# One inverse moved to GpSimd, the later pairs' scans put off by one pair, and a block of MLP pieces placed ahead of the fifth pair

## The chip, the core and the metric

The kernel runs on one core of one Trainium2 chip. The metric is the device time of one execution in microseconds. The engines are named as the profile names them: PE (TensorE; PEld is its weight load), DVE (VectorE), ACT (ScalarE), POOL (GpSimd) and SP (SyncE, which issues most transfers). Each engine takes its instructions in the order in which they stand in its own queue.

## The reference: a recurrence and two MLPs

Inputs are six arrays r, k, v, w, a, b of 4 batches x 8 heads x 768 steps x 40. Per batch and head a 40 x 40 state is carried over the steps:

```python
y[t]  = r[t] @ state
Sa    = state @ a[t]
state = state * w[t][None, :] - outer(Sa, b[t]) + outer(v[t], k[t])
```

The outputs y of all heads are joined to x (3072 tokens x 320). The first MLP normalises x by its root mean square, computes `silu(xn @ w_gate) * (xn @ w_val) @ w_out` with an inner width of 1536. The second computes `(h - tanh(h)) @ w_out2` with `h = x @ w_in2` and an inner width of 2048. All is float32.

## The kernel before: pairs of chunks, an inverse per group of pairs, MLP pieces in between

**Recurrence.** The 768 steps are cut into chunks of 64. A unit is one batch and one chunk (all 8 heads); two units make a pair, and there are 24 pairs, counted here from 0, so that "the fifth pair" is pair 4. A loop `for p in range(NP + 1)` (L826) goes over the pairs. In each turn of it PE computes the right-hand side (`emit_rhs`, L397), the outputs of the pair before (`emit_y`, L505 and L507), the first solve (`emit_u`, L408), a correction (`emit_w`, L417; DVE adds it at L418), the second solve (`emit_u2`, L425) and then the state's update and the products for the output. A solve multiplies by TT, the inverse of a triangular 64 x 64 matrix that is loaded by `load_t` (L347).

**What has to be there before a solve.** A unit's inputs are loaded into the arena (`load_p`, L203); DVE runs two scans over them (`emit_p`, L218 and L222), POOL makes three products (L228 to L230), and they are spilled (L234). `emit_m` (L247) then makes the pair's matrices on PE, which go to DRAM as `md`. Pairs are inverted in groups: (0,1), (2,3), (4,5), (6,7), (8 to 11), (12 to 15), (16 to 19), (20 to 23), here group 0 to group 7. `inverse` loads a group's matrices from `md` (L270), runs 31 steps of two instructions each, a product into tmp (L276) and a subtraction (L278), which makes 62 instructions, each needing the one before, and stores the result as `td` (L282). `load_t` reads `td`. Groups 0, 1 and 3 run on DVE, the others on POOL. All groups but group 1 (tile mt) use the same place in the arena. When a group's last pair has its matrices, `m_due` puts its inverse into `held`, and it is run at the end of that turn of the loop. A dictionary `AHEAD` says which pairs' scans are begun in which turn: before, pairs 4, 5, 6 in turns 0, 1, 2, then two pairs in each of the turns 3 to 5, and p + 7 from then on. At turn 18 and later a turn that has no inverse in `held` begins splits of the second MLP's weights (`some2`).

**Weights.** Products are made of rounded high and low parts. `split_words` splits a block of 128 rows of weights: an absolute value on ACT, five instructions on DVE (L141, L142, L143, L145, L146), a copy on ACT, two on POOL (L150, L151). The first MLP has 48 such blocks (6 chunks of 8), the second 40. The tile fa, which a block holds from ACT's first instruction to POOL's last one, has three buffers; raw, the words as loaded, has four.

**First MLP.** It runs in 12 blocks of 256 tokens, one for every two pairs, cut into pieces: an up piece (8 matmuls at L556; two make one of 12 slices f) and a down piece (6 matmuls, L561 to L563, per f, two slices behind). `moe(RATE)` (L768) is called about nine times in a turn and puts in as many pieces as its credit allows. Where no block is ready it puts in 8 matmuls on a tile of zeros instead, which are called fillers here (`warm`, L288). A block can begin when its two pairs have been normalised (`emit_x1`: ACT, POOL at L516 and L517, DVE at L518, POOL at L519; stored to DRAM), loaded again and transposed (`emit_x2`).

**What sets the order.** PE's order is written out by the program as it stands. The order on DVE, ACT, POOL and SP comes from a list scheduler: each instruction gets a priority (`when`, `step`, `later`), and the scheduler places it by its own reckoning of times. What stands in a queue is therefore fixed before the run, and an instruction that has to wait holds all that stand behind it.

Of the kernel before, what the change touches and what calls it, by code (L numbers as in the profile page):

```python
# [20 lines left out]
HC = C // 2  # L21
NCH = S // C
NU = B * NCH
NP = NU // 2
# [5 lines left out]
UNITS = [(b0 + g, c) for b0 in range(0, B, G) for c in range(NCH) for g in range(G)]  # L30
GROUPS = [(g, g + 2) for g in range(0, 8, 2)] + [(g, g + 4) for g in range(8, NP, 4)]

AHEAD = {3: (7, 8), 4: (9, 10), 5: (11, 12)}
KEEP = 2
NPO = 6
NPE = 8
NRAW = 4
NFA = 3
EARLY1 = 2
# [19 lines left out]
AR_P = HC * HC * 2  # L59
# [9 lines left out]
def wkv_chunks__then__gated_mlp__then__tanh_mlp_kernel(  # L69
# [269 lines left out]
    def load_t(p):  # L339
        if p >= NP:  # L340
            return
        gi = group_of[p]
        x = p - GROUPS[gi][0]
        for s in range(2):
            for h in range(2):
                r0 = 64 * s + 32 * h
                SP.dma_start(out=TT[r0:r0 + HC, :, :, 32 * h:32 * h + HC].rearrange("p w q t -> p (w q) t"),  # L347
                             in_=td_d[gi][h, x, s].rearrange("w q j t -> j (w q) t"))
# [277 lines left out]
    with tc.manual_schedule(engines={mybir.EngineType.PE}):  # L626
# [30 lines left out]
        mt = fp.tile([128, AR_P], F32, tag="mt", name="mt")  # L657

        with tc.manual_schedule(engines={ET.DVE, ET.SP, ET.Activation, ET.Pool}):
            when(-100)  # L660
            for u in range(4):
                load_p(u, fp)
            SP.dma_start(out=idn, in_=ident)
            SP.dma_start(out=msk, in_=masks[1:2].rearrange("o p t -> p o t"))
            for u in range(4, NPO):
                load_p(u, fp)
            DVE.memset(z65, 0.0)
            DVE.memset(z65[:, :, 0:1], 1.0)
            DVE.memset(zr, 0.0)
            for t in (turn[0], turn[1], gapped, solve, wz):  # L670
                DVE.memset(t, 0.0)
            i0 = inverse(0, DVE, MA, TA, fp)
            i1 = inverse(1, DVE, mt[:, 0:HC * HC], mt[:, HC * HC:AR_P], fp)
            next(i0)
            POOL.memset(EP, 0.0)
            POOL.memset(cm05, -0.5)
            for u in range(4):
                emit_p(u, fp)
                if u % 2:
                    emit_m(u // 2, fp)  # L680
            for t in (Q, VS, UV, MX, TT):
                DVE.memset(t, 0.0)
            POOL.memset(RU, 0.0)
            load_kl(0)
            load_q(0)
            load_v(0)
            load_r(0)
            next(i0)
            load_mx(0)
            for u in range(6, 8):  # L690
                load_p(u, fp)
            emit_s(0)
            emit_p(4, fp)
            emit_p(5, fp)
            for w in range(2):
                emit_kb(0, w)
            load_e(0)
            next(i1)
            for k in range(HC - 1):
                if k == 8:  # L700
                    emit_mak(0)
                if k == 18:
                    emit_rhs(0)
                next(i0)
            emit_m(2, fp)
            spill_p(4, SP)
            run(i0)
            first_w = lastd[0]
            load_t(0)
            spill_p(5, SP)  # L710
            warm(WARM0)
            emit_p(6, fp)
            emit_p(7, fp)
            SP.dma_start(out=gB, in_=rms_g.rearrange("(o n) -> o n", o=1).to_broadcast([128, DM]))
            spill_p(6, SP)
            spill_p(7, SP)
# [109 lines left out]
        for p in range(NP + 1):  # L826
            period[0] = p
            now, more = p < NP, p + 1 < NP
            if now:
                scans.extend(2 * q + w for q in AHEAD.get(p, (p + 4 if p < 3 else p + 7,)) if q < NP for w in range(2))  # L830
            if p == 1:
                for u in range(2 * KEEP):
                    po_t.pop(u)
                    sp_t.pop(u)
                last_t = lastd[0]
                first.close()
                w1p = phA.enter_context(tc.tile_pool(name="w1p", bufs=1, side="right", reuse_waits="tile"))
                with tc.issue_after(last_t.ins):
                    prep1(range(EARLY1, KF1 // 2), w1p)
                when(vt[0])  # L840
                pairs.close()
                ma = phA.enter_context(tc.tile_pool(name="ma", bufs=2, side="right", reuse_waits="tile"))
            if now and p:
                emit_rhs(p)
                load_q(p + 1)
            if p:
                emit_y(p - 1)
                load_r(p)
                later(X_LATE, emit_x1, p - 1)
            step(1.8)  # L850
            moe(RATE)
            if now:
                emit_u(p)
                if p == 0:
                    load_q(1)
                    emit_m(3, fp)
                    when(0)
                    run(i1)
                    when(vt[0])
                else:  # L860
                    m_due()
                step(1.2)
                moe(RATE)
                emit_w(p)
                if more:
                    if p + 1 not in kl_t:
                        load_kl(p + 1)
                    load_mx(p + 1)
                    emit_kb(p + 1, 0)
                stage_p()  # L870
                step(1.2)
                moe(RATE)
                emit_u2(p)
                emit_ut(p)
                load_t(p + 1)
                if more:
                    emit_kb(p + 1, 1)
                step(1.9)
                moe(RATE)
                emit_d(p)  # L880
                load_v(p + 1)
                stage_p()
                step(0.8)
            if p > 1:
                x2()
                step(0.5)
            moe(RATE)
            if now:
                for w in range(2):
                    emit_z(p, w)  # L890
                    step(0.8)
                    moe(RATE)
                if more:
                    emit_mak(p + 1)
                    if p + 2 < NP:
                        load_kl(p + 2)
                    emit_s(p + 1)
                if scans:
                    m_due()
                    stage_p()  # L900
                step(1.5)
                moe(RATE)
                emit_e(p)
                load_e(p + 1)
                if scans:
                    stage_p()
                step(0.4)
            if p > 1:
                x2()
                step(0.5)  # L910
            moe(RATE)
            if held:
                with tc.issue_after(gate[0].ins), tc.issue_after(gate_pool[0].ins):
                    later(I_LATE, run, held.pop(0))
            elif p >= 18:
                some2()
        with tc.issue_after(gate[0].ins), tc.issue_after(gate_act[0].ins):
# [130 lines left out]
```

## Time and profile before

| | us |
|---|---|
| median of 2 runs (1435.42 to 1435.57) | 1435.49 |
| the profiled execution's own time | 1433.76 |
| its span from the first to the last instruction | 1432.0 |
| PE busy in the span | 1233.9 |
| DVE busy | 717.1 |
| POOL busy | 707.7 |
| ACT busy | 469.4 |

The span leaves 1.76 us of the profiled execution's time outside it, and the execution is 1.73 us under the median of the runs. In a row of the timeline stand the start, the time taken, engine, source line, operation, tiles written and read, shapes and count; in square brackets how long the engine sat idle before, and what ended that. A row of the groups has the busy time, the mean of one in ns, and the idle time before. Instructions of one engine that follow each other closely can overlap in a row of matmuls, since their ends are modelled.

### The profile page before, as it was taken

Reading aid. Unit: us, or ns where it says so; the run is one execution under the profiler, and the core shown is the slowest. Engines: PE = TensorE matmul, PEld = TensorE weight load, DVE = VectorE, ACT = ScalarE, POOL = GpSimd, SP = SyncE. Lnnn points to the kernel's source line nnn. Section 1 sums busy time; section 2 is a strip of 40 time slices with the busy share of each in tenths; the row PEclk is TensorE's granted clock in tenths of the full one; section 3 lists DMA queues with packets and bytes.
Section 4 is the critical chain, followed back from the end, with each engine's and each line's share of the span. In section 5 each row is a group of like instructions: output and inputs, shape, how many; then the busy total and the mean of one; then the engine's idle time right before and its main releaser. Section 6 shows DMA issues by size and latency. Waiting matters only on the chain.

```text
span 1432.0 us, 35619 instructions
## 1 busy us (share of the span) xinstructions
PE 1233.9 (86%) x14676; PEld 1139.0 (80%) x14676; DVE 717.1 (50%) x1487; ACT 469.4 (33%) x1077; POOL 707.7 (49%) x1049
## 2 busy tenths in 40 slices
PE   2666676279889989998999899998877999999997
PEld 1555566278789979998999898988766999899997
DVE  5989899563434434443443344435978222222221
ACT  1132332123223323333333233333434333333332
POOL 5554788533683395349425622324767333333332
PEclk9888678589999999999999999999999999999999
DMA  8476765444755645565544334332331101010000
GB/s 211 103 178 155 183 183 160 113 129 121 187 131 136 155 122 159 132 144 130 145 124 92 97 80 113 93 94 72 98 106 53 24 23 30 12 41 20 1 19 19
DMA packets 208421, 149.95 MB, mean 105 GB/s; under 512 B 132962, under 2 KB 182338, under 8 KB 208258
## 3 DMA queue, kind: packets, MB, share of 16 engines
q1 hardware_dynamic: 182914, 141.38, 38.1%
q10 hardware_dynamic: 25344, 6.29, 2.1%
q8 instruction: 115, 1.88, 0.6%
q14 instruction: 48, 0.39, 0.1%
HBM read 106.01 MB, written 41.62 MB: 103 GB/s over the span
## 4 chain that ended last, share of the span: by engine, by line
PE 59%; DVE 18%; POOL 9%; DMA 7%; issue 5%; SPq 1%; ACT 1%; ACTq 0%; DVEq 0%; POOLq 0%
PE ups L556 26%; PE acc L561 6%; PE acc L563 6%; PE acc L562 6%; DVE fa L143 3%; POOL arena L278 3%; PE turn L482 2%; POOL tmp L276 2%; DVE fa L141 2%; DVE raw L146 2%; DVE fa L142 2%; DVE raw L145 1%; DVE tmph L276 1%; POOL hl L584 1%; PE solve L425 1%
## 5 line engine op out<-in xcount | busy, mean ns | idle before, releaser
L556 PE MATMUL ups<-xh,w1c 128*128 128x256 f32 x1440 | 235.5, 295 | 11.0 <-ACT xh L544 5.7
L969 POOL TENSOR_TENSOR hl<-th,hh 128x512 fp32r<-128x512 f32 x96 | 124.4, 1297 | 206.9 <-ACT hh L968 205.0
L584 POOL TENSOR_TENSOR hl<-hf,hh 128x256 fp32r<-128x256 f32 x144 | 110.7, 768 | 217.2 <-ACT hh L583 212.1
L556 PEld LDWEIGHTS ups<-xh,w1c 128*128 128x128 f32 x1440 | 199.1, 196 | 17.5 <-ACT xh L544 8.1
L965 DVE TENSOR_TENSOR th<-ups,th 128x512 f32<-128x512 f32 x96 | 66.3, 690 | 229.3 <-ACT th L964 229.3
L556 PE MATMUL ups<-xl,w1c 128*128 128x256 f32 x864 | 154.0, 288 | 8.1 <-DVE xl L545 8.1
L578 DVE SCALAR_TENSOR_TENSOR th<-th,ups 128x256 f32<-128x256 f32 x144 | 59.8, 415 | 197.7 <-ACT th L577 197.3
L556 PEld LDWEIGHTS ups<-xl,w1c 128*128 128x128 f32 x864 | 127.5, 196 | 8.5 <-DVE xl L545 8.5
L583 ACT CAST hh<-hf 128x256 fp32r<-128x256 f32 x144 | 58.4, 406 | 194.0 <-DVE hf L580 192.3
L556 PE MATMUL ups<-yh,w2c 128*128 128x512 f32 x360 | 102.6, 396 | 2.2 <-DVE th L965 2.2
L561 PE MATMUL acc<-w1c,hh 128*128 128x320 f32 x288 | 95.9, 333 | 5.8 <-ACT xo L598 5.2
L964 ACT ACTIVATE th<-ups 128x512 f32<-128x512 f32 x96 | 57.1, 595 | 131.1 <-PE ups L556 130.5
L563 PE MATMUL acc<-w1c,hl 128*128 128x320 f32 x288 | 92.0, 319 | 8.6 <-POOL hl L584 8.5
L577 ACT ACTIVATE th<-ups 128x256 f32<-128x256 f32 x144 | 55.1, 383 | 123.3 <-PE ups L556 106.6
L276 POOL TENSOR_TENSOR tmp<-arena 128x31 f32<-128x31 f32 (+23 forms) x155 | 78.0, 503 | 26.6 <-DMA arena<-md 18.1
L562 PE MATMUL acc<-w1c,hh 128*128 128x320 f32 x288 | 90.5, 314 | 0.0
L561 PE MATMUL acc<-w2c,hh 128*128 128x320 f32 x288 | 86.9, 312 | 3.6 <-ACT hh L968 3.6
L278 POOL TENSOR_TENSOR arena<-arena,tmp 128x31 f32<-128x31 f32 (+23 forms) x155 | 83.0, 535 | 9.0
L562 PE MATMUL acc<-w2c,hh 128*128 128x320 f32 x288 | 87.2, 312 | 0.0
L968 ACT CAST hh<-th 128x512 fp32r<-128x512 f32 x96 | 59.6, 621 | 73.8 <-DVE th L965 61.4
L408 PE MATMUL solve<-RS,TT 64*64 64x40 f32 x768 | 32.0, 240 | 56.0 <-DMA TT<-td 51.2
L288 PE MATMUL wps<-wz 128*128 128x256 bf16 x516 | 78.7, 307 | 0.0
(157 smaller groups left out, 2906.2 us busy)
## 6 DMA issues: line engine op xcount, KB each, us to landing
arena<-in_abkw_dram SPq DMA_DIRECT2D x40, 418.0 KB
sp<-arena SPq DMA_DIRECT2D x40, 417.6 KB
RU<-in_vr_dram SPq DMA_DIRECT2D x48, 312.0 KB
kl<-sp SPq DMA_DIRECT2D x22, 416.0 KB
raw<-in_w_out_dram SPq DMA_DIRECT2D x28, 320.0 KB
md<-ms ACTq DMA_DIRECT2D x48, 128.0 KB
xd<-XS SPq DMA_DIRECT2D x24, 192.0 KB
xin<-xd SPq DMA_DIRECT2D x24, 192.0 KB
```

Source lines behind the costliest of these rows:

```text
L276: eng.tensor_tensor(out=tv, in0=T[:, :nr, s:s + 1].to_broadcast([128, nr, wd]), in1=M[:, s:s + 1, s + 1:HC].to_broadcast([128, nr, wd]), o ...
L278: lastd[0] = eng.tensor_tensor(out=T[:, :nr, s + 1:HC], in0=T[:, :nr, s + 1:HC], in1=tv, op=ALU.subtract)
L288: PE.matmul(wp[:, 0].rearrange("p (a b) -> p a b", a=2), lhsT=wz[:, 0], rhs=wz.to_broadcast([128, 2, 128]), start=True, stop=True)
L556: PE.matmul(ps, lhsT=l, rhs=r[:, :n], start=i == 0, stop=i == 7)
L561: PE.matmul(acc[t][:, :DM], lhsT=hh[:, c], rhs=oh, start=f == 0, stop=False)
L562: PE.matmul(acc[t][:, :DM], lhsT=hh[:, c], rhs=ol, start=False, stop=False)
L563: PE.matmul(acc[t][:, :DM], lhsT=hl[:, c], rhs=oh, start=False, stop=f == nf - 1)
L578: DVE.scalar_tensor_tensor(out=th, in0=th, scalar=1.0, in1=ps[:, 0], op0=ALU.add, op1=ALU.mult)
L584: POOL.tensor_tensor(out=hl, in0=hf, in1=hh, op=ALU.subtract)
L965: DVE.tensor_tensor(out=th, in0=ps, in1=th, op=ALU.subtract)
L968: ACT.copy(hh, th)
L969: POOL.tensor_tensor(out=hl, in0=th, in1=hh, op=ALU.subtract)
```

## The change

It has four parts.

1. The inverse of group 1 (pairs 2 and 3) is made on POOL, not on DVE.
2. `AHEAD` begins the scans of every pair from 4 on one turn later: none in turn 0, pair 4 in turn 1, and p + 6 from turn 7 on.
3. At the begin of turn 4, ahead of that turn's right-hand side, `moe` is called 12 times with a credit of 34/12 each.
4. `load_t(4)` moves from the second solve of turn 3 to the end of turn 3, behind the inverse that is then run.

```diff
-AHEAD = {3: (7, 8), 4: (9, 10), 5: (11, 12)}
+AHEAD = {0: (), 1: (4,), 2: (5,), 3: (6,), 4: (7, 8), 5: (9, 10), 6: (11, 12)}
 KEEP = 2
 NPO = 6
 NPE = 8
+PAUSE = 34.0
...
             i0 = inverse(0, DVE, MA, TA, fp)
-            i1 = inverse(1, DVE, mt[:, 0:HC * HC], mt[:, HC * HC:AR_P], fp)
+            i1 = inverse(1, POOL, mt[:, 0:HC * HC], mt[:, HC * HC:AR_P], fp)
...
             if now:
-                scans.extend(2 * q + w for q in AHEAD.get(p, (p + 4 if p < 3 else p + 7,)) if q < NP for w in range(2))
+                scans.extend(2 * q + w for q in AHEAD.get(p, (p + 6,)) if q < NP for w in range(2))
...
+            if p == 4:
+                for _ in range(12):
+                    moe(PAUSE / 12)
             if now and p:
                 emit_rhs(p)
                 load_q(p + 1)
...
                 emit_ut(p)
-                load_t(p + 1)
+                if p != 3:
+                    load_t(p + 1)
...
                     later(I_LATE, run, held.pop(0))
+                if p == 3:
+                    load_t(4)
```

What the scheduler makes of it is shown at two places. The first is the end of group 1's inverse (tile mt; XS and ss belong to the normalisation of a pair's outputs, RS to a pair's right-hand side, fa to a split). Before, on DVE, around the right-hand side of pair 2:

```order
L276 TENSOR_TENSOR tmph_949<-mt_203 128x45
L278 TENSOR_TENSOR mt_203<-mt_203,tmph_949 128x15x3
L276 TENSOR_TENSOR tmph_952<-mt_203 128x30
L399 TENSOR_SCALAR RS_186<-turn1_163 64x320
L278 TENSOR_TENSOR mt_203<-mt_203,tmph_952 128x15x2
L276 TENSOR_TENSOR tmph_955<-mt_203 128x16
L278 TENSOR_TENSOR mt_203<-mt_203,tmph_955 128x16
L141 TENSOR_SCALAR fa_1209<-fa_1209 128x256
```

Now, on POOL (line numbers of the changed kernel are 1 larger here):

```order
L517 TENSOR_SCALAR ss_1960<-ss_1960 128x1
L277 TENSOR_TENSOR tmph_940<-mt_203 128x78
L518 TENSOR_TENSOR ss_1960<-ss_1960,cm05_180 128x1
L279 TENSOR_TENSOR mt_203<-mt_203,tmph_940 128x13x6
L277 TENSOR_TENSOR tmph_943<-mt_203 128x70
L520 COPY XS_190<-XS_190 128x64
L279 TENSOR_TENSOR mt_203<-mt_203,tmph_943 128x14x5
L277 TENSOR_TENSOR tmph_946<-mt_203 128x56
L279 TENSOR_TENSOR mt_203<-mt_203,tmph_946 128x14x4
```

The last nine instructions of the inverse stand behind the normalisation of pair 1, whose outputs PE makes right after pair 2's right-hand side; six instructions follow the piece shown, and then the splits' products go on. The second place is SP's queue where pair 8 needs the inverse of group 4 (td4; xd7 is the store of pair 7's normalised outputs, MX, RU, VS and Q are inputs of a pair). Before:

```order
L528 DMA xin_5060<-xd6_118 128x384
L355 DMA MX_188<-md4_100 32x8x32 x2
L234 DMA sp14_86<-arena_170 104x1028
L203 DMA arena_170<-in_abkw_dram 104x1029
L282 DMA td4_108<-arena_170 128x1024
L321 DMA UV_184<-in_vn_dram 64x2x320
L347 DMA TT_187<-td4_108 32x8x32 x4
```

Now:

```order
L318 DMA VS_183<-in_vn_dram 64x2x160
L327 DMA RU_185<-in_vr_dram 104x4x192 x2
L521 DMA xd7_119<-XS_190 128x384
L529 DMA xin_5657<-xd7_119 128x384
L283 DMA td4_108<-arena_170 128x1024
L348 DMA TT_187<-td4_108 32x8x32 x4
L235 DMA sp14_86<-arena_170 104x1028
```

Before, the store of the inverse stood ahead of the store of pair 7's outputs by most of a turn (the outputs of pair 7 are made in turn 8). Now it stands behind it, and the load for pair 8's solve follows directly. On POOL the last 18 of group 4's 62 inverse instructions stand behind the normalisation of pair 7, and 17 of them also behind the low part (hl) of an MLP slice whose two up pieces PE runs between pair 7's outputs and pair 8's solve.

On PE, whose order the program writes out itself, 16 up and 10 down pieces (all that is left of block 0) and then 5 fillers now stand ahead of turn 4's right-hand side. Turn 4 has 5 up pieces and 7 fillers where it had 14 up and 8 down pieces, turn 6 has 9 up, 5 down and 3 fillers where it had 12, 6 and 2; from turn 7 on the pieces are the same.

## The prediction

> **What bounds the kernel now.** First the page's slices of 35.8 us, then stretches, then the first solve of each pair on PE, then DVE's groups while the first MLP's weights are split.
>
> ```profile
> span 1432.0 us, 35619 instructions
> PE   2666676279889989998999899998877999999997
> DVE  5989899563434434443443344435978222222221
> ```
>
> PE is full from about 320 us on, except near 1000 us; in both gaps DVE is full instead. The stretches (busy times in the order PE, PEld, DVE, ACT, POOL, then the granted clock) say it in us:
>
> ```profile
> 100.00:150.00 50.00, 31.88 (x585) 27.86 (x584) 44.60 (x114) 13.81 (x35) 26.98 (x37) 0.80 0.61 155
> 200.00:250.00 50.00, 34.62 (x488) 31.62 (x486) 49.31 (x85) 16.55 (x43) 40.95 (x59) 0.88 0.65 174
> 1000.00:1100.00 100.00, 78.35 (x470) 70.76 (x469) 86.81 (x173) 41.55 (x103) 66.58 (x76) 0.93 0.32 97
> ```
>
> PE's timeline (L397 is a right-hand side, L408 a first solve, L425 a second):
>
> ```profile
> 101.39 1.13 PE L397 MATMUL turn<-VS,Q 128*64 128x40 f32 x32 [0.71 <-DVE Q L387]
> 117.65 1.93 PE L425 MATMUL solve<-RS,TT 64*64 64x40 f32 x32 [4.16 <-DVE RS L418]
> 133.31 1.13 PE L397 MATMUL turn<-VS,Q 128*64 128x40 f32 x32 [0.73 <-issue]
> 146.83 2.18 PE L408 MATMUL solve<-RS,TT 64*64 64x40 f32 x31 [9.54 <-DMA TT<-td]
> 275.67 0.40 PE L408 MATMUL solve<-RS,TT 64*64 64x40 f32 x2 [34.19 <-DMA TT<-td]
> 328.80 1.13 PE L408 MATMUL solve<-RS,TT 64*64 64x40 f32 x32
> 414.54 1.13 PE L408 MATMUL solve<-RS,TT 64*64 64x40 f32 x32
> 449.53 1.13 PE L408 MATMUL solve<-RS,TT 64*64 64x40 f32 x32
> 517.09 1.13 PE L408 MATMUL solve<-RS,TT 64*64 64x40 f32 x32
> 589.49 0.72 PE L408 MATMUL solve<-RS,TT 64*64 64x40 f32 x18
> ```
>
> These are turns 1 (its right-hand side and second solve) and 2, then the solves of pairs 4, 5, 7, 8, 10 and 12. Pair 2 waits 9.5 us for group 1's inverse, pair 4 34.2 us for group 2's. Pairs 8 and 12 wait for nothing.
>
> **Up to the solve of pair 4: +3.** DVE's groups from 50 to 260 us, POOL's inverse of group 2 in the same time, and three single rows:
>
> ```profile
> L146 DVE SCALAR_TENSOR_TENSOR raw<-raw 128x256 f32<-128x256 uint32 (+1 forms) x48 | 30.1, 634 | 0.7
> L145 DVE TENSOR_SCALAR raw<-fa 128x256 int32<-128x256 int32 (+1 forms) x48 | 18.9, 402 | 0.6
> L276 DVE TENSOR_TENSOR tmph<-mt 128x126 f32<-128x126 f32 (+22 forms) x31 | 11.9, 383 | 0.5
> L278 DVE TENSOR_TENSOR mt<-mt,tmph 128x126 f32<-128x126 f32 (+22 forms) x31 | 9.5, 308 | 0.6
> L218 DVE TENSOR_TENSOR_SCAN sx<-arena,z 104x260 f32<-104x260 f32 x11 | 10.9, 991 | 0.0
> L222 DVE TENSOR_TENSOR_SCAN arena<-arena,zr 104x260 f32<-104x260 f32 x11 | 10.1, 922 | 0.1
> ...
> L278 POOL TENSOR_TENSOR arena<-arena,tmp 128x126 f32<-128x126 f32 (+22 forms) x31 | 13.6, 440 | 1.5
> L276 POOL TENSOR_TENSOR tmp<-arena 128x126 f32<-128x126 f32 (+22 forms) x31 | 12.9, 417 | 1.4 <-DMA arena<-md 0.2
> ...
> 275.12 0.19 DVE L276 TENSOR_TENSOR tmp<-arena 128x31 f32<-128x31 f32 x1 [15.34 <-DMA arena<-md]
> ...
> 269.10 1.28 SPq L282 DMA_DIRECT2D td<-arena  x2
> ...
> 444.51 1.13 PE L397 MATMUL turn<-VS,Q 128*64 128x40 f32 x32
> 450.25 0.24 POOL L519 COPY XS<-XS 128x64 f32<-128x64 f32 x1 [0.65 <-DVE XS L518]
> 452.53 0.74 POOL L584 TENSOR_TENSOR hl<-hf,hh 128x256 fp32r<-128x256 f32 x1
> ```
>
> DVE ends the first weights' splits at 275.12 - 15.34 = 259.8. It loses group 1's inverse, 11.9 + 9.5 = 21.4 us, and by then four units' scans, 4 x (0.99 + 0.92 + 0.17 for a reciprocal, estimated) = 8.3 us. But the inverse on POOL ends behind pair 1's normalisation. A normalisation ends on POOL 5.7 us after its turn's right-hand side starts (444.51 to 450.25), nine inverse instructions at 0.43 take 3.9, and from the store of an inverse to the solve it took 6.6 us (269.10 to 275.67). Pair 2's right-hand side comes sooner by the 4.16 us for which the second solve waited for DVE, at 129.2; so its solve is at 129.2 + 5.7 + 3.9 + 6.6 = 145.4, against 146.8: nothing gained there. Until the inverse ends, 138.8, the next split has no free fa buffer, because the products that free it stand behind the inverse on POOL. From 101.4 on DVE then has 37 us for 19 split instructions at 0.52 (middle of 402 and 634 ns), one unit's scans and some 13 others at about 0.5: 19 us, so 18 idle, where the row of 100 to 150 us has 4 in 37: +14. Splits end at 259.8 - 21.4 - 8.3 + 14 + 1.6 (two more MLP slices, 0.4 us an instruction) = 245.7.
>
> The block ahead of pair 4 is not 34 us of work. Only block 0 is ready, so PE gets 16 up and 10 down pieces and then 5 fillers. Four slices come after the last split: about 8 us, to 254. Behind the last slice's hl stand 31 inverse instructions of group 2 on POOL, 13.3 us, with pair 3's normalisation between them, about 5 with its waits; with the 6.6 pair 4 solves at 279, against 275.7. **+3** (-12 to +15, from the idle time of DVE).
>
> **Turns 4 to 6: -19.** Pieces and a filler as PE ran them, and two waits of these turns:
>
> ```profile
> 622.78 0.31 PE L561 MATMUL acc<-w1c,hh 128*128 128x320 f32 x1
> 623.67 0.76 PE L556 MATMUL ups<-xh,w1c 128*128 128x256 f32 x5
> 624.71 1.13 PE L417 MATMUL turn<-U,MX 64*64 64x40 f32 x32
> ...
> 126.06 1.04 PE L288 MATMUL wps<-wz 128*128 128x256 bf16 x8
> ...
> 319.60 1.01 PE L556 MATMUL ups<-xl,w1c 128*128 128x256 f32 x3 [5.75 <-DVE xl L545]
> 397.53 0.63 PE L563 MATMUL acc<-w1c,hl 128*128 128x320 f32 x1 [3.03 <-POOL hl L584]
> ```
>
> A down piece takes 0.89 us, an up piece 1.04. By PE's order 12 up and 9 down pieces now lie ahead of pair 4's solve that came in turns 4 to 6, which get 8 fillers more: -12.5 - 8.0 + 8.3 = -12. The inverse of group 4 and its waits leave these turns, and a lighter PE gives DVE time: of 5.75 + 3.03 I take 7 off. Before, 275.67 to 414.54 is 138.9 us; now 120 (112 to 129). Pair 7 solves at 399.
>
> **Turn 7: +22.** Group 4's inverse is one turn later, its reader is not.
>
> ```profile
> 355.55 1.12 PE L247 MATMUL turn<-arena 40*64 40x64 f32 x32
> 430.27 0.35 SPq L282 DMA_DIRECT2D td<-arena  x1
> 548.94 0.35 SPq L282 DMA_DIRECT2D td<-arena  x1
> ```
>
> From pair 11's matrices to the store took 74.7 us, in turns 5 to 7. Now these matrices come about 11 us ahead of pair 7's solve, so the same length would put pair 8's solve at 74.7 - 11 + 6.6 = 70 us after pair 7's, where it was 35.0. The least is given by the order: pair 8's right-hand side, its neighbour hl done 8.8 us later (444.51 to 453.27), 17 inverse instructions, 7.3, and 6.6: 22.7, where it was 5.0. That is 17.7; I take 22, nearer to the least because POOL has fewer hl to wait for.
>
> **Turns 11 and 15: +5.** Group 5's store (548.94) stood 40.6 us ahead of pair 12's solve. A turn is 36 (517.09 to 589.49 are two), and 6.6 are needed: 2 us late, and the load now stands behind the next pair's inputs on SP, 3 more. Groups 6 and 7 had more room: 0 (together 0 to 12).
>
> **From turn 18: +5.** Group 7's inverse still stands in `held` at turn 18, so the second MLP's splits begin a turn later and two blocks more fall into the stretch near 1000 us, where DVE is 87% busy: 10 instructions x 0.52 (0 to 8).
>
> Sum: 3 - 19 + 22 + 5 + 5 = **+16** on the profiled execution's own 1433.76, that is 1450; the median of the runs lies 1.7 above that execution, which I leave in the range.
>
> One measured pair of rows speaks against moving the inverse. Group 3's inverse, of the same shapes, on DVE with POOL nearly still:
>
> ```profile
> L276 DVE TENSOR_TENSOR tmp<-arena x31: 171/257/643, 275.1 to 298.6; 128x126 f32<-128x126 f32 x3, 128x30 f32<-128x30 f32 x2, 128x56 f32<-128x56 f32 x2, 128x78 f32<-128x78 f32 x2
> ```
>
> Its median is 257 ns, where group 1's beside POOL's splits had a mean of 383. The Trainium skill (SBUF — State Buffer, "Who interferes with whom") says that a DVE instruction with two SBUF inputs contends with a GpSimd instruction that reads SBUF, and that the second to issue blocks until the first has finished; the two rows agree. By that rule the inverse taken off DVE could come back as blocking, which is the second rival.
>
> **Rivals.**
> - *The gain arrives* (0.22). DVE fills its idle time, splits end at 234, turns 4 to 6 save 28, and only the least is paid at pair 8: -12 - 28 + 18 + 2 + 2 = -18, 1416 (1398 to 1432). For it: DVE is the bound of 50 to 250 us. Against: the order of POOL at pairs 2 and 8.
> - *POOL blocks DVE* (0.16). 62 instructions at 0.43 are 26.6 us of POOL; if half of it holds DVE up, splits end 13 later and pair 4 with them: +29, 1463 (to 1476). It decides if the splits end after about 255.
> - *Every inverse is late* (0.09), the slower end: the 74.7 us hold at pair 8 (+35), pairs 12 and 16 wait 12 and 8 us because one turn is less than an inverse with its transfers needs: 3 - 19 + 35 + 20 + 5 = +44, 1478 and more. It decides when an inverse's store comes after its reader's right-hand side.
> - The change could also do nothing in sum; that lies inside the first two.
>
> **Numbers.** Forecast 0.53, 1438 to 1463. The range 1412 to 1474 leaves out about a third of the first rival and the last one. A measurement tells apart what differs by over 2%, 28.7 us: faster (under 1406.8) a third of the first rival, 0.07; slower (over 1464.2) half of the second and the third, 0.17; within, 0.76.
>
> **What would show it.** In the profile after: the waits of L408 at pairs 2 (about 11 us), 4 (about 15) and 8 (18 to 24) with TT<-td as releaser; POOL's last write to mt about 10 us behind L397; DVE's last L146 on w1c at 246; 120 us from pair 4's solve to pair 7's. If pair 8 does not wait, or the splits end before 235, the forecast is wrong on the fast side; if pairs 12 and 16 wait over 10 us each, on the slow side.

## The result: slower by 2.7%, and the profile after

| | before | after |
|---|---|---|
| median of 2 runs, us | 1435.49 | 1474.12 (1473.18 to 1475.05) |
| ratio, 95% interval | | 1.0269, 1.0225 to 1.0313 |
| the profiled execution's own time | 1433.76 | 1473.18 |
| its span | 1432.0 | 1471.4 |

The forecast was 1450, with a range of 1412 to 1474. The page of the changed kernel gives the slices, now of 36.8 us each:

```profile
PE   2675678697994998899899999999588999999997
...
DVE  5783997167451443345344333445969322222221
```

DVE has a hollow in slice 4 (3 where it was at 9), and is done in slice 8 (1 for 5), where PE is fuller than before (6 for 2). The largest loss shows in slice 13, where PE falls from 9 to 4. For the rest the slices are too coarse. PE's timeline of the changed kernel, with the first solves (L409, one line further down than before) of pairs 2, 4, 6, 7, 8, 12 and 16, is the view that carries the result:

```profile
145.76 0.41 PE L409 MATMUL solve<-RS,TT 64*64 64x40 f32 x2 [13.71 <-DMA TT<-td]
281.03 0.41 PE L409 MATMUL solve<-RS,TT 64*64 64x40 f32 x2 [11.34 <-DMA TT<-td]
366.49 2.27 PE L409 MATMUL solve<-RS,TT 64*64 64x40 f32 x31 [6.88 <-DMA TT<-td]
403.50 0.31 PE L409 MATMUL solve<-RS,TT 64*64 64x40 f32 x2
463.62 0.40 PE L409 MATMUL solve<-RS,TT 64*64 64x40 f32 x2 [19.46 <-DMA TT<-td]
613.13 0.41 PE L409 MATMUL solve<-RS,TT 64*64 64x40 f32 x2 [4.16 <-DMA TT<-td]
759.86 0.28 PE L409 MATMUL solve<-RS,TT 64*64 64x40 f32 x2 [2.17 <-DMA TT<-td]
```

Pair 4's wait has shrunk from 34.19 to 11.34 us, and yet its solve comes 5.4 us later. Pairs 6, 8, 12 and 16, which had not waited for an inverse, now wait for that of their group. Against the first solves of before, the span's +39.4 us come together like this: up to pair 4 +5.4; turns 4 to 6 -16.4 (122.5 for 138.9); turn 7 +25.1 (60.1 for 35.0); turns 8 to 22 +23.0 (533.7 for 510.6); the rest +2.3.

The waits alone are too small for the +23.0. The stretches of turns 8 and 12 of the changed kernel (busy us of PE, PEld, DVE, ACT and POOL with their counts, then the clock granted to TensorE, then the DMA engines' busy share and GB/s, which are not used here) show what stands behind them:

```profile
463.60:499.20 35.60, 33.91 (x509) 31.78 (x509) 12.99 (x24) 10.03 (x24) 8.04 (x15) 0.89 0.41 106
613.10:648.00 34.90, 33.40 (x479) 31.25 (x479) 12.72 (x24) 10.29 (x25) 8.68 (x16) 0.88 0.58 153
```

And turn 8 before:

```profile
449.50:480.70 31.20, 30.60 (x512) 28.55 (x511) 14.22 (x27) 10.62 (x26) 9.05 (x18) 1.00 0.61 154
```

PE runs as many matmuls in turn 8 as before (509 and 512) and needs 4.4 us more, 3.3 of them busy, at a mean clock of 0.89 where it was 1.00. Microseconds around pair 12's solve in the changed kernel, in the same columns, show where the clock goes:

```profile
611.10:612.10 1.00, 0.00 (x0) 0.00 (x0) 0.14 (x1) 0.00 (x0) 0.74 (x2) 0.61 0.54 115
612.10:613.10 1.00, 0.00 (x0) 0.00 (x0) 0.97 (x3) 0.00 (x0) 0.24 (x1) 0.50 0.43 67
613.10:614.10 1.00, 0.59 (x6) 0.51 (x8) 0.20 (x1) 0.41 (x1) 0.23 (x1) 0.50 0.19 30
...
620.10:621.10 1.00, 1.00 (x6) 1.00 (x6) 0.18 (x1) 0.00 (x0) 1.00 (x2) 0.50 0.94 219
621.10:622.10 1.00, 1.00 (x9) 1.00 (x7) 0.00 (x0) 0.00 (x0) 0.30 (x1) 0.77 1.28 306
```

PE is idle for 4.16 us; the granted clock falls to half while it waits and comes back only at about 621.6, so the first 8.4 us of work run at half speed, which is 4.2 us more if all of it takes twice as long. The turn took 4.6 more than before (34.8 for 30.2).

### The profile page after: what moved, and what is told of

The parts are those of the page before. It is cut to its first block, busy times and chain, and to the rows that moved or that the text cites. A ratio compares the mean times of both kernels' runs of the same rounds, so it can differ in the third digit from the quotient of the medians.

```text
span 1471.4 us, 35865 instructions
## 1 busy us (share of the span) xinstructions
PE 1260.9 (86%) x14788; PEld 1160.6 (79%) x14788; DVE 697.1 (47%) x1425; ACT 469.7 (32%) x1077; POOL 730.2 (50%) x1111
## 4 chain that ended last, share of the span: by engine, by line
PE 54%; DVE 17%; POOL 11%; DMA 8%; issue 6%; SPq 2%; ACT 1%; ACTq 0%; POOLq 0%; DVEq 0%
PE ups L557 23%; PE acc L564 5%; PE acc L562 5%; PE acc L563 5%; POOL arena L279 3%; POOL tmp L277 3%; DVE fa L144 3%; DVE fa L142 2%; PE turn L483 2%; DMA arena<-md 2%; DVE raw L147 2%; DVE fa L143 2%; PE solve L409 2%; POOL hl L585 1%; PE wps L289 1%
## 5 line engine op out<-in xcount | busy, mean ns | idle before, releaser
L557 PE MATMUL ups<-xh,w1c 128*128 128x256 f32 x1440 | 236.6, 296 | 17.4 <-DVE hf L581 10.1
L562 PE MATMUL acc<-w1c,hh 128*128 128x320 f32 x288 | 97.5, 339 | 5.7 <-ACT xo L599 4.9
L409 PE MATMUL solve<-RS,TT 64*64 64x40 f32 x768 | 36.7, 252 | 73.9 <-DMA TT<-td 68.4
L289 PE MATMUL wps<-wz 128*128 128x256 bf16 x628 | 96.1, 308 | 0.0
L409 PEld LDWEIGHTS solve<-RS,TT 64*64 64x64 f32 x768 | 32.7, 161 | 78.9 <-issue 69.7
L563 PE MATMUL acc<-w1c,hh 128*128 128x320 f32 x288 | 92.0, 320 | 0.0
## 6 DMA issues: line engine op xcount, KB each, us to landing
md<-ms ACTq DMA_DIRECT2D x48, 128.0 KB
```

The source lines that it names most:

```text
L289: PE.matmul(wp[:, 0].rearrange("p (a b) -> p a b", a=2), lhsT=wz[:, 0], rhs=wz.to_broadcast([128, 2, 128]), start=True, stop=True)
L409: PE.matmul(sol[r, w, q], lhsT=TT[r, w, q], rhs=RS[r, w, q], start=True, stop=True)
L557: PE.matmul(ps, lhsT=l, rhs=r[:, :n], start=i == 0, stop=i == 7)
L562: PE.matmul(acc[t][:, :DM], lhsT=hh[:, c], rhs=oh, start=f == 0, stop=False)
L563: PE.matmul(acc[t][:, :DM], lhsT=hh[:, c], rhs=ol, start=False, stop=False)
```

## The experiments

The table has the profiled executions of all kernels, in us, read from the first solves as above; "own" is the profiled execution's own time.

| kernel | own | pair 4 solves | turns 4-6 | turn 7 | turn 8 | pair 9 to end |
|---|---|---|---|---|---|---|
| before | 1433.8 | 275.7 | 138.9 | 35.0 | 31.2 | 951.3 |
| changed | 1473.2 | 281.0 | 122.5 | 60.1 | 35.6 | 972.2 |
| changed, once more (e0) | 1472.4 | 283.8 | 120.0 | 59.7 | 35.7 | 971.4 |
| e1: part 1 alone | 1434.6 | 289.5 | 128.2 | 35.0 | 31.2 | 949.0 |
| e2: parts 2 and 4 | 1480.9 | 274.0 | 136.4 | 61.7 | 36.1 | 970.8 |
| e3: part 3 alone | 1420.7 | 285.8 | 116.1 | 36.5 | 31.7 | 948.9 |
| e4: changed, fillers ahead of three solves | 1471.5 | 285.7 | 120.2 | 62.4 | 31.6 | 969.7 |
| e5: changed, later groups on time | 1462.1 | 288.4 | 122.3 | 66.7 | 35.5 | 947.4 |
| e6: e5, and groups of two up to pair 11 | 1439.6 | 284.7 | 124.7 | 43.0 | 37.3 | 948.1 |
| e7: changed without part 1 | 1469.2 | 281.7 | 119.1 | 60.4 | 36.6 | 969.6 |
| e8: parts 3 and 4 | 1417.0 | 282.0 | 116.6 | 36.8 | 31.2 | 948.7 |
| e9: e6 without part 1 | 1436.6 | 277.6 | 128.0 | 45.8 | 34.8 | 948.6 |

The early turns scatter: e0 has the changed kernel's order and solves pair 4 2.8 us later, and e4, with the same order up to there, 4.7. Medians and intervals are given with each run.

### Part 1 alone: group 1's inverse on POOL

Against the kernel before:

```diff
-            i1 = inverse(1, DVE, mt[:, 0:HC * HC], mt[:, HC * HC:AR_P], fp)
+            i1 = inverse(1, POOL, mt[:, 0:HC * HC], mt[:, HC * HC:AR_P], fp)
```

> Only part 1: group 1's inverse on POOL, all else as before. Theory A (the loss sits in the inverses that the later scans put a turn later, at pairs 8, 12 and 16; the early part gains): no wait of pairs 8, 12, 16 for TT; pair 2 solves at 144 to 148 us as in both kernels, the splits on DVE end at about 253 instead of 259.8, pair 4 solves at 266 to 272, and the whole takes 1424 to 1436 us. Theory B (POOL's inverse blocks DVE through the shared port, and the loss is made there): splits end at 262 or later, 1440 us or more.

Measured: 1433.36, ratio 1.0003 (0.9986 to 1.0021). DVE's last split and pair 4's solve in this run, and then ACT's copy of the splits that comes behind group 1's inverse, before and in this run:

```profile
273.31 0.57 DVE L146 SCALAR_TENSOR_TENSOR raw<-raw 128x320 f32<-128x320 uint32 x1
...
289.52 0.40 PE L408 MATMUL solve<-RS,TT 64*64 64x40 f32 x2 [33.50 <-DMA TT<-td]
```

```profile
141.41 1.02 ACT L147 CAST w1c<-fa 128x256 fp32r<-128x256 f32 x3 [1.57 <-DMA td<-mt]
```

```profile
152.10 1.02 ACT L147 CAST w1c<-fa 128x256 fp32r<-128x256 f32 x3 [11.60 <-DMA td<-mt]
```

The total was in the range of the first theory, but not for its reason: pair 2 solves at 154.5, not at 144 to 148, the splits end 14 us later than before, not earlier, and pair 4 solves 14 us later. That the splits end behind 262 is what theory B named, but not for its reason: the mean of L146 is 613 ns here against 634 before, so that instruction was not held up longer. By the trace the copy into w1c (L147) waits in both kernels until the store of the inverse from mt has landed. The program says why: the room of mt is given up (`first.close()`), and the weights of the later chunks are put into the same place (`w1p`). The inverse ends on POOL at 148.4, where DVE was done at 137.1, and the three splits at hand, and with them DVE, wait for it. By pair 8's solve (452.67 for 449.53) all but 3 us has been won back, 11 of them in turns 4 to 6. With 21 us less to do, DVE finished later, and it cost next to nothing.

### Parts 2 and 4 alone: the later scans

Against the changed kernel:

```diff
-            i1 = inverse(1, POOL, mt[:, 0:HC * HC], mt[:, HC * HC:AR_P], fp)
+            i1 = inverse(1, DVE, mt[:, 0:HC * HC], mt[:, HC * HC:AR_P], fp)
...
-            if p == 4:
-                for _ in range(12):
-                    moe(PAUSE / 12)
```

> Parts 2 and 4 without 1 and 3: scans of pairs 4 and up a turn later, load_t(4) behind its inverse; group 1's inverse on DVE, no pieces ahead of pair 4. Theory A: pair 8 waits 15 to 22 us for TT, pairs 12 and 16 a few us each, and from pair 7's solve to the end it takes 1068 us as in the changed kernel (1017.5 before); pair 7 solves at about 410, so 1472 to 1485 us in all. Theory C (the later scans cost little by themselves, the pieces ahead of pair 4 or POOL's inverse do it): under 1455 us.

Measured: 1475.9, ratio 1.0311 (1.0278 to 1.0343). Pairs 4 and 8:

```profile
274.04 0.40 PE L409 MATMUL solve<-RS,TT 64*64 64x40 f32 x2 [45.35 <-DMA TT<-td]
...
472.17 0.40 PE L409 MATMUL solve<-RS,TT 64*64 64x40 f32 x2 [18.61 <-DMA TT<-td]
```

The whole loss is in these two parts, of which part 4 has no effect without part 2 (below); part 2 without part 4 was not tried. They give 1.6 us at pair 4 and 2.5 in turns 4 to 6, and cost 26.7 in turn 7, 5.0 in turn 8 and 19.5 from pair 9 on.

### Part 3 alone: the block of pieces ahead of pair 4

Against the kernel before:

```diff
+            if p == 4:
+                for _ in range(12):
+                    moe(34.0 / 12)
```

> Only part 3: the 12 calls of moe ahead of turn 4's right-hand side, all else as before. Theory A: pair 4 solves at about 284 (275.7 before), because the pieces wait for the last splits and the normalisation of pair 3 for the pieces; about 20 us of pieces then lie ahead of it, 8 more fillers behind; no wait at pairs 8, 12, 16; 1424 to 1440 us. Theory C: 1450 us or more.

Measured: 1420.27, ratio 0.9917 (0.9889 to 0.9945), the best of all, 4 us below the range that was expected, and faster than the kernel before by less than 1%. The stretch up to pair 4's solve, before and then in this run, in the columns above:

```profile
230.00:275.70 45.70, 10.02 (x139) 9.51 (x139) 29.48 (x52) 8.46 (x24) 33.66 (x61) 0.64 0.59 146
```

```profile
230.00:285.70 55.70, 41.36 (x430) 38.18 (x426) 39.99 (x79) 15.31 (x41) 40.69 (x71) 0.93 0.47 119
```

And the solves of pairs 4 and 8 in it:

```profile
285.75 0.40 PE L408 MATMUL solve<-RS,TT 64*64 64x40 f32 x2 [3.53 <-DMA TT<-td]
438.41 1.13 PE L408 MATMUL solve<-RS,TT 64*64 64x40 f32 x32
```

PE works 31 us more in the hole before pair 4, and the mean granted clock there is 0.93 instead of 0.64. Pair 4 comes 10.1 us later, turns 4 to 6 take 22.8 less, and from pair 5 on no solve waits for an inverse, so that pair 8 is 11.1 us ahead of before. So the gain of turns 4 to 6 that the changed kernel shows is mainly this part's.

### Fillers ahead of the three late solves

```diff
+            for _ in range({8: 21, 12: 6, 16: 4}.get(p, 0)):
+                warm(8)
```

These lines stand ahead of the first solve in the changed kernel; each call adds 8 matmuls on zeros.

> The changed kernel with fillers on PE straight ahead of the first solve of pair 8 (21 groups of 8), 12 (6) and 16 (4), about 18.5, 5.3 and 3.5 us of work in the place of the waits of 19.5, 4.2 and 2.2 us; no other work is changed. Theory K (after each wait PE runs some 9 us at half the granted clock, which makes turns 8, 12 and 16 4.5 to 4.7 us longer than before): these turns take 31, 30 and 31 us again, the granted clock in them is 1.00, and the whole takes 1458 to 1464 us. Theory L (these turns are longer because transfers or POOL's products come late behind the inverse): turns stay at 35 us, 1472 to 1477 us.

Measured: 1467.14, ratio 1.0251 (1.0223 to 1.028). Nine microseconds from the solves of pairs 8, 12 and 16:

```profile
468.30:477.30 9.00, 9.00 (x156) 8.59 (x156) 3.32 (x6) 2.13 (x5) 4.57 (x7) 1.00 0.49 100
617.90:626.90 9.00, 9.00 (x156) 8.57 (x156) 3.33 (x6) 2.13 (x5) 4.57 (x7) 1.00 0.65 163
763.00:772.00 9.00, 9.00 (x157) 8.62 (x157) 3.31 (x6) 2.13 (x5) 4.57 (x7) 1.00 0.63 156
```

The clock stays at 1.00, and turns 8, 12 and 16 take 31.6, 30.7 and 31.2 us, within 0.5 of before (31.2, 30.2, 30.9). So of the 4.5 to 4.7 us that each of these turns had lost, 4.0 to 4.4 come back when PE is kept busy through the wait. The fillers, with pauses of 2.95 and 1.59 us among those of pairs 8 and 12, lasted longer than the waits, however: turns 7, 11 and 15 took 2.3, 2.9 and 1.4 us more than in the changed kernel (62.4, 41.9 and 39.6), which gave half of it back. The time is therefore 3 us above the 1458 to 1464 expected, and the ratio is not told apart from the changed kernel's; the turns carry this result, not the total.

### Later groups' scans on time again

Against the changed kernel:

```diff
-AHEAD = {0: (), 1: (4,), 2: (5,), 3: (6,), 4: (7, 8), 5: (9, 10), 6: (11, 12)}
+AHEAD = {0: (), 1: (4,), 2: (5,), 3: (6,), 4: (7, 8), 5: (9, 10), 6: (11, 12), 7: (13, 14)}
...
-                scans.extend(2 * q + w for q in AHEAD.get(p, (p + 6,)) if q < NP for w in range(2))
+                scans.extend(2 * q + w for q in AHEAD.get(p, (p + 7,)) if q < NP for w in range(2))
```

> Theory A (the inverses of groups 4 to 7, begun one turn later than before, are the whole loss behind pair 8: the waits at pairs 12 and 16 and the stretch at half clock behind each): with groups 5 to 7 begun in the turn in which they were begun before, the waits at pairs 12 and 16 are gone, turns 12 and 16 take 30 to 32 us, and from pair 9's solve to the end of the span it is 951 to 957 us (before 951.3, changed kernel 972.2). Pair 8 still waits 15 to 21 us. Time 1451 to 1460. Rival B (the loss behind pair 8 comes from the work that the early turns put off, on whichever engine, and not from the inverses): the waits go but the turns are longer elsewhere, 965 us or more from pair 9 to the end, time 1467 or more.

Measured: 1459.56, ratio 1.0175 (1.0153 to 1.0197); the changed kernel on the same chip 1472.85, 1.0272 (1.0248 to 1.0296).

> The changed kernel as it is, on the same chip as the three others, to set them against. Both theories expect 1470 to 1478, pair 8 to wait 17 to 21 us, pair 12 3 to 5 and pair 16 1.5 to 3; the solve of pair 4 may move by some 5 us, as it did between two programs with the same order in these turns.

The solves of pairs 8, 9 and 12 in the run with the scans on time:

```profile
477.41 0.40 PE L409 MATMUL solve<-RS,TT 64*64 64x40 f32 x2 [23.77 <-DMA TT<-td]
512.90 1.13 PE L409 MATMUL solve<-RS,TT 64*64 64x40 f32 x32
620.52 1.13 PE L409 MATMUL solve<-RS,TT 64*64 64x40 f32 x32
```

The waits at pairs 12 and 16 are gone, and from pair 9 to the end it is 947.4 us, even less than before's 951.3. So theory A holds for all that lies behind pair 9: late inverses, with the half clock behind them, and no other loss that this run shows. Pair 8 missed the expectation: it waits 23.8, not 15 to 21, and turn 7 is 7 us longer. Turn 7 now begins the scans of two pairs (13 and 14) instead of one, and their products come to POOL while it makes group 4's inverse; that this is the cause was not tried.

### And pairs 8 to 11 in groups of two

Against the kernel of the experiment before:

```diff
-GROUPS = [(g, g + 2) for g in range(0, 8, 2)] + [(g, g + 4) for g in range(8, NP, 4)]
+GROUPS = [(g, g + 2) for g in range(0, 12, 2)] + [(g, g + 4) for g in range(12, NP, 4)]
```

> As the run before, and pairs 8 to 11 are inverted as (8, 9) and (10, 11), so that pair 8's inverse has to wait for pairs 8 and 9 alone. Theory A (pair 8 waits because its inverse cannot begin before pair 11's matrices): the wait at pair 8 is under 3 us, turn 7 takes 35 to 42 us, from pair 7's solve to the end of the span it is 1017 to 1030 us (before 1017.5, changed kernel 1067.9), and the time is 1421 to 1436. Rival C (the gain of turns 4 to 6 is only lent: the pieces and the inverse that left them have to be run later, whatever pair 8 waits for): turns 4 to 6 are 130 us or more, or from pair 7 to the end it is 1035 us or more, time 1441 or more.

Measured: 1447.18 (1439.58 to 1448.45), ratio 1.0078 (1.0047 to 1.0109). The solve of pair 8, and then the stretches of turns 7 and 8:

```profile
452.43 1.13 PE L409 MATMUL solve<-RS,TT 64*64 64x40 f32 x32
```

```profile
409.40:452.40 43.00, 39.21 (x578) 37.68 (x577) 20.02 (x40) 13.19 (x34) 32.10 (x73) 0.92 0.69 167
452.40:489.70 37.30, 33.81 (x510) 31.12 (x509) 14.42 (x27) 10.74 (x26) 22.69 (x54) 0.91 0.54 139
```

Pair 8 waits for nothing, and turn 7 is 17 us shorter than in the changed kernel. So its wait came from the group of four, whose inverse can't begin before pair 11's matrices. From pair 7's solve to the end it is 1028.4 us, within theory A's range. Still, turn 7 is a microsecond above it, turns 7 and 8 take 80.3 us in sum, 14.2 more than before, and the median is in theory C's range (the profiled execution is the fastest of four, 7.6 us below the median). Of the 14.2 us, 6.7 are idle time of PE (7.3 us, before 0.6; the longest waits are 3.2 us for DVE's xl in turn 7 and 2.4 for POOL's hl in turn 8), and half of the 13.7 us at half clock in these turns is another 6.8. In the turn 8 of before that is shown above, POOL was busy for 9.05 us; here for 22.69, with the inverse of pairs 10 and 11, one more than before. That this is why xl and hl come late is likely, but was not tried. In the sum of turns 4 to 8 the later scans with the block of pieces take 205.0 us, as before, and part 3 alone takes 184.3: though neither of theory C's two stretches came out as it said, its point that the gain is given back holds.

### The changed kernel without part 1, and with both mendings

The same edit against the changed kernel and against the one with groups of two:

```diff
-            i1 = inverse(1, POOL, mt[:, 0:HC * HC], mt[:, HC * HC:AR_P], fp)
+            i1 = inverse(1, DVE, mt[:, 0:HC * HC], mt[:, HC * HC:AR_P], fp)
```

> The changed kernel without its first part: group 1's inverse is on DVE again. Theory A (the first part gives and takes about the same: pair 2 waits less, the splits end later): pair 2 waits 4 to 10 us, pair 3 solves 5 to 10 us earlier than in the changed kernel, the splits end at 250 to 258, pair 4 solves within 6 us of the changed kernel's 281.0, pair 8 still waits 15 to 21, and the time is 1468 to 1480. Rival D (the first part is what costs: the inverse on POOL holds the splits' products back): pair 4 solves at 272 or before and the time is 1464 or less.

> The changed kernel with the two mendings (groups of two up to pair 11, scans begun on time from turn 7 on) and with group 1's inverse on DVE again. Theory A (put off scans lend time to turns 4 to 6 and have to pay it back in turns 7 and 8; the inverse on POOL costs some 5 us more): 1438 to 1446, pair 8 waits less than 3 us, turns 7 and 8 take 74 us or more in sum (before 66.2). Rival F (the 80 us of these two turns come from the inverse on POOL through the later splits): turns 7 and 8 under 70 us, 1434 or less.

Measured: 1468.0, ratio 1.023 (1.0206 to 1.0255), for the first; 1434.7, 1.0019 (1.0002 to 1.0035), for the second. In the first, pair 3 solves at 185.3, 9.8 us earlier than in the changed kernel on the same chip, DVE's last split ends at 254.8, and pair 4 solves at 281.7, only 2.1 earlier. So part 1 costs about 5 us by the medians, 3 by the spans. Those 3 lie 2.1 at pair 4, which is within the scatter of the early turns, and the rest spread over the later turns; their cause was not found. In the second, turns 7 and 8 take 80.6 us, as with the inverse on POOL: the payback there does not come from part 1. Its time is 3 us below the first theory's range; part 1 costs 0.6% there (1.0078 against 1.0019, two sets of runs), 3 us by the spans.

### Parts 3 and 4 together

Against the kernel before:

```diff
+            if p == 4:
+                for _ in range(12):
+                    moe(34.0 / 12)
...
-                load_t(p + 1)
+                if p != 3:
+                    load_t(p + 1)
...
+                if p == 3:
+                    load_t(4)
```

> The kernel before with the third and the fourth part and without the first two. Theory A (the third part is the only one that gains, the fourth does nothing by itself): 1416 to 1425, ratio 0.988 to 0.995, as the third part alone measured, and no solve waits from pair 5 on. Rival E (the third part's 0.8% was the scatter of the early turns, which differ by some 5 us between programs with the same order): 1429 or more, an interval that reaches 1.

Measured: 1420.51, ratio 0.992 (0.9899 to 0.9941). On every engine the instructions stand in the same order as with part 3 alone (in the trace eight matmuls start in exchanged order, as 14 do between two executions of the changed kernel), so this is that kernel a second time: the gain of 0.8% is not the scatter of the early turns. The fourth part without the second moves nothing.

With group 1's inverse on DVE the parts add up. Parts 2 and 4 +3.11%, part 3 -0.83%, together +2.28%, where the changed kernel without part 1 measured +2.30%; part 1 adds 0.42 to that (2.72 against 2.30 on one chip). Against the kernel before it added only 0.03, so what it costs depends on the order that it is put into.

## Why the prediction was wrong, step by step

**Up to pair 4: +3, measured +5.4, right in its dates, with one link missing.** Pair 2 solves at 145.76 (145.4 was worked out) behind a wait of 13.7, where about 11 was named. POOL's last write to mt and DVE's last split in the changed kernel, with ACT's copy between them, and then the stretch in which DVE idles:

```profile
139.51 0.23 POOL L279 TENSOR_TENSOR mt<-mt,tmph 128x16 f32<-128x16 f32 x1
...
143.47 1.02 ACT L148 CAST w1c<-fa 128x256 fp32r<-128x256 f32 x3 [11.14 <-DMA td<-mt]
...
245.80 0.69 DVE L147 SCALAR_TENSOR_TENSOR raw<-raw 128x320 f32<-128x320 uint32 x1
```

```profile
100.00:150.00 50.00, 29.51 (x556) 26.10 (x556) 24.68 (x53) 11.07 (x28) 38.16 (x73) 0.83 0.52 129
```

The inverse ends at 139.7 (138.8 expected), the splits at 246.5 (245.7), and DVE is busy for 24.7 us of the 50 where it was 44.6. What DVE waits for is not what was named, though. The prediction had the products on POOL hold the fa buffers, because they stand behind the inverse. By the trace those products wait for ACT's copy into w1c, and the copy waits for the store of the inverse, whose place the new weights take, 3.7 us beyond the inverse's end. The idle time came out near all the same: DVE was busy for 21.0 us of the 37, where 19 were expected. The splits end 13 us earlier and pair 4 gets nothing of it, because group 2's inverse stands on POOL behind the last hl. That holds for parts 1 and 2 together only. The same steps for part 1 alone said 266 to 272 for pair 4, and it was 289.5: by itself the inverse on POOL ended at 148.4, not 138.8, and the splits ended later. What the step had worked out from rows of before was right for one order and not for another, and the +5.4 itself is hardly more than the 4.7 by which pair 4's solve scatters.

**Turns 4 to 6: -19, measured -16.4, with one wait missing.** Pieces were to give 12, and a lighter PE 7 through shorter waits. These turns before, in the changed kernel and with part 3 alone:

```profile
275.67:414.54 138.87, 119.60 (x1686) 113.11 (x1687) 70.53 (x165) 37.19 (x91) 66.52 (x116) 0.89 0.50 130
```

```profile
281.03:403.50 122.47, 108.41 (x1632) 100.19 (x1632) 68.11 (x156) 30.99 (x75) 41.62 (x69) 0.86 0.61 156
```

```profile
285.75:401.87 116.12, 106.93 (x1600) 98.79 (x1600) 65.76 (x149) 31.76 (x77) 56.98 (x100) 0.87 0.62 161
```

With part 3 alone PE's busy time falls by 12.7 us and its idle time by 10.1 (from 19.3 to 9.2), which makes the 22.8: the pieces gave what was named, and the waits more. The clock is not behind it, at 0.89 before and 0.87 here. In the changed kernel the busy time falls by 11.2 and the idle time by only 5.2. The waits for xl and hl shrink from 9.0 us to 1.0, but 7.6 us of waits for an inverse are new, 6.88 of them at pair 6 for group 3's, which no step had.

**Turn 7: +22, measured +25.1.** The wait of 19.46 lies in the 18 to 24 expected, close to the 17.7 that the order gave as the least, and it is the group's: with groups of two it is gone. What makes 25.1 of it is a wait of 2.26 us of pair 7's solve for DVE and the half clock behind that:

```profile
406.50:413.30 6.80, 6.80 (x71) 6.68 (x68) 1.37 (x5) 2.43 (x7) 3.95 (x11) 0.50 0.67 126
```

Half of these 6.8 us is 3.4, and 19.5 + 2.3 + 3.4 is 25.1 with rounding. So the 22 came near by its allowance over the least, and not because the cause of the rest was seen.

**Turns 11 and 15: +5, measured +23.0 over turns 8 to 22. This is the step that failed.** It counted group 6 as not late, though its store before (685.63) stood 41.9 us ahead of pair 16's solve (727.52), only 1.3 more than group 5's ahead of pair 12's. For the waits the 5 was not far off: 4.16 us at pair 12 and 2.17 at pair 16, turns 11 and 15 longer by 5.4 and 3.1, together 8.5. What was missing is what a wait does to PE behind it. Each of the three solves that waited was followed by half clock, and turns 8, 12 and 16 were 4.5, 4.6 and 4.7 us longer, 13.8 in sum. By the clock's own records half of the time at half clock in these turns is 3.9, 4.2 and 3.4 us; a second wait for the same load, behind the first two matmuls of the solve, adds 0.58, 0.37 and 0.66. The prediction had the clock's rows in hand (0.80, 0.88 and 0.93 in its stretches) and put the clock at nothing in every term. The kernel before shows the price too, in turn 10, where pair 10's second solve waits and half clock follows:

```profile
530.42 1.93 PE L425 MATMUL solve<-RS,TT 64*64 64x40 f32 x32 [4.85 <-DVE RS L418]
```

```profile
529.40:536.20 6.80, 5.78 (x75) 5.62 (x76) 0.93 (x3) 3.16 (x7) 6.41 (x11) 0.50 0.81 223
```

That turn took 38.8 us, where turn 16 with the same 509 matmuls, and no such wait, took 30.9: 7.9 more for a wait of 4.85. The waits' 8.5 and these 13.8 make 22.3 of the 23.0; the remaining 0.7 are small differences in turns 9, 10 and 14. The run with the scans on time took back all of it behind pair 9, the one with fillers 12.5 of the 13.8.

PE's right-hand sides of pairs 12 and 16 in the changed kernel, and the stores of the inverses that their solves need:

```profile
603.88 1.13 PE L398 MATMUL turn<-VS,Q 128*64 128x40 f32 x32
...
752.59 1.13 PE L398 MATMUL turn<-VS,Q 128*64 128x40 f32 x32
```

```profile
606.07 0.36 SPq L283 DMA_DIRECT2D td<-arena  x1
...
753.06 0.35 SPq L283 DMA_DIRECT2D td<-arena  x1
```

Both stores come just behind the right-hand sides, with a load still to follow.

**From turn 18: +5, measured +2.3**, inside its 0 to 8. The step isn't shown by that: from pair 23's solve to the end, the kernel before took 471.8 us and part 1 alone 469.4, which is as large a difference.

**The rivals.** That the gain arrives failed at pair 8 and pair 6. That every inverse is late had 0.09, and its mechanism is what the turns show: the stores come behind their readers' right-hand sides, the point from which it was to decide, and 8.5 us more in turns 11 and 15 with 9.3 more in turns 12 and 16 make 17.8 of its 20. That number was luck, since its 20 was made of waits of 12 and 8 us and of no clock. Its +35 for pair 8 was too much (25.1, and 4.5 in turn 8). The sign that was named for it, waits of over 10 us each at pairs 12 and 16, did not come, because the cost of a short wait is mostly not in the wait. That POOL blocks DVE had 0.16. The row that spoke for it set the median of group 3's products on DVE, 257 ns, against the mean of group 1's, 383. Like with like the medians are 257 and 248 ns, and the means 264 and 383; for the subtractions the means are 323 and 308. So the two groups differ in a few long products (up to 1536 ns) alone. The split instruction that was costliest on DVE before, in the changed kernel, from 50 to 260 us as before:

```profile
L147 DVE SCALAR_TENSOR_TENSOR raw<-raw 128x256 f32<-128x256 uint32 (+1 forms) x48 | 27.7, 583 | 0.5
```

Its mean is 583 ns, against 634 before, but the scans around it were moved too. Where the place of the inverse is the only difference, the five split instructions on DVE take 2.60 us a block with it on POOL and 2.45 with it on DVE (the changed kernel again, and without part 1), which is 7 us over the 48 blocks; in the kernels with groups of two it is 5 us, and against the kernel before 1.6. So DVE's instructions did get longer, by well under the 13 us of this rival and the 21.4 us of inverse that DVE lost, and the splits ended at 246.5, ahead of the 255 from which it was to decide. The Trainium skill (SBUF — State Buffer, "Who interferes with whom") says that of a DVE instruction with two SBUF inputs and a GpSimd instruction that reads SBUF, the second to issue blocks. That rule is not shown by these means: most of the difference is in an instruction with one tensor as input (L143, 504 ns against 412), and no run separates the causes.

## What to carry to other kernels

Before work is put off, look for who reads what it makes, and how long the chain behind it is: here DVE's scans were the first link of a chain over PE, DRAM, POOL and SP, and what kept PE from waiting was its slack. Less the 6.6 us from store to solve, the stores of groups 4 to 7 stood 12.7, 34.0, 35.3 and 42.9 us ahead of their solves before, and a turn takes about 36: put off by one turn, groups 4, 5 and 6 were late, and group 7 was not. Price a new wait on PE with the slow clock that can stand behind it: here waits of 2.2, 4.2 and 19.5 us each were followed by a turn some 4.6 us longer. Fill a hole on the waiting engine with work that has to be done anyway, as the third part does, and try each part of a change by itself: the one that gained 0.8% was hidden under one that lost 3.1%.

## What the runs showed of the hardware that was not expected

A wait of 2.17 us (pair 16) was enough to bring the half clock. Microseconds of the changed kernel around it:

```profile
758.80:759.80 1.00, 0.00 (x0) 0.00 (x0) 0.12 (x1) 0.00 (x0) 0.75 (x2) 1.00 0.45 69
759.80:760.80 1.00, 0.28 (x2) 0.22 (x3) 0.97 (x3) 0.00 (x0) 0.24 (x1) 1.00 0.32 36
760.80:761.80 1.00, 1.00 (x30) 1.00 (x31) 0.21 (x1) 0.00 (x0) 0.00 (x0) 0.85 0.67 177
761.80:762.80 1.00, 1.00 (x23) 1.00 (x23) 0.00 (x0) 0.64 (x2) 0.00 (x0) 0.50 0.43 118
...
767.80:768.80 1.00, 1.00 (x9) 0.86 (x8) 0.00 (x0) 0.00 (x0) 0.44 (x1) 0.74 1.00 219
```

The clock was still 1.00 when PE began again at 759.86, fell some 1.6 us later, with PE busy, and was full again at about 768.3, 6.8 us after it fell. That is 8.4 us behind PE's new begin, as at pair 12, where the clock had fallen during the wait. The length of the idle time alone does not decide it: PE idled for 2.23 us at 1083.89 in the kernel before, for 2.28 at 1046.51 in the changed one and for 2.95 among the fillers at 448.69, and the clock stayed at 1.00. The Trainium skill (TensorE: Matmul & The Clock Gate, "Part 1: The HAM clock gate (the "warmup" mystery)") says that the clock falls to half after at least one idle window of about 3.4 us and comes back after about 3.4 us of sustained work. The trace agrees with the two levels and differs here in both lengths: 2.17 us of idle time, with 0.28 us of work in the microsecond behind it, were enough at pair 16, and full speed was back only 8.4 us after PE had begun again, at full clock for the first 1.6 of them there and at half clock throughout at pair 12. What sets these lengths was not tried.

The same order of instructions does not always give the same early turns: two profiled executions of the changed kernel solve pair 4 at 281.0 and 283.8, and the kernel with fillers, which has the same order up to there, at 285.7. Differences of that size in these turns carry nothing.
